# Head of a mixer kernel: one x tile ahead of w1, two tiles through DMA transposes, second products as single groups

## The chip, the cores and the metric

The kernel runs on one core of a Trainium2 chip. The metric is the device time of one execution in microseconds (us). The time before is 138.96 us, the median of 3 runs (138.89 to 139.11). A core has five engines that run side by side, each through its own list of instructions in order: TensorE (PE; its weight loads are listed as PEld), VectorE (DVE), ScalarE (ACT), GpSimd (POOL) and SyncE (SP), whose queue issues nearly all DMAs here. They wait for each other through semaphores.

## The reference

x has 2048 rows (tokens) of 512 numbers, in bf16.

```python
h  = gelu(layernorm(x) @ w1)                  # 512 -> 512
c  = 128                                      # four channel groups, each shifted along the rows
g0 = h[:, :,   0:128] shifted down by 1 row   # zeros come in at the end
g1 = h[:, :, 128:256] shifted up by 1
g2 = h[:, :, 256:384] shifted down by 2
g3 = h[:, :, 384:512] shifted up by 2
x1 = x + concat(g0, g1, g2, g3) @ w2          # 512 -> 512
out = x1 + gelu(layernorm(x1) @ w3) @ w4      # 512 -> 1792 -> 512
```

## The kernel before, in words

**Tiles.** Row 16p + t of x lies in partition p of tile t, so there are 16 tiles of 128 rows, and a shift by one row is a step to the next tile (at the ends also by one partition, for which a few columns of zeros are kept). All of x, of the weights and of the intermediate results stays on the chip.

**First layer.** For a tile, VectorE takes the statistics (step `st`, line 328) and aggregates them to mean and variance (`ag`, 331); GpSimd makes 1/sqrt(variance + eps) by a power (`rs`, lines 354 and 363, for two tiles at once); VectorE normalizes the tile to bf16 (`norm`, 434). Tile 2 is an exception: ScalarE sums it and its squared deviations (`sum`, `dev`, lines 378 and 390), and `vp`, `vpd` and `pw` (lines 407, 399, 414) make its factor and tile 3's. The normalized tile has to be transposed. Either TensorE does it, four 128 by 128 transposes into a PSUM bank (`tp`, 456) and an evacuation to `xT` by ScalarE (`evA`, 468) or VectorE (`evD`, 470); or a DMA transpose, issued by SyncE, does it from SBUF to SBUF (`dT`, 444). Before, tiles 0 to 7 go through TensorE and 8 to 15 through the DMA. The product with w1 (`m1`, 507) is made for pairs of tiles, one or more of the four output groups at a time; tiles 0 and 1 go one by one and input chunk by input chunk (`m1x`, 524), so that they can begin with the first half of w1. ScalarE applies the gelu (`g1`, lines 551 to 568) and writes `hT`, four channel groups with tiles side by side.

**Second product.** `m2 t b j...` (line 582) multiplies, for output tile t into PSUM bank b, the shifted window of channel group j with its rows of w2; four groups j add up in the bank. Tile t wants the gelus of tiles t - 2 to t + 2. VectorE adds x (`add`, 594).

**Second layer.** Statistics, factor, normalization (on ScalarE for the first ten tiles, 424) and a DMA transpose for each tile of x1, in the order 2, 3, ..., 15, 0, 1. Then, for four tiles at a time, the wide product with w3 (line 609, output 1792, gelu at 622) and the narrow one with w4 (line 635), an addition of x1 (649) and the store (653).

**Order.** Nothing is scheduled automatically: the program's steps are recorded in the order of a text, `HEAD`, and of the calls behind it, and each engine runs its instructions in just this order. A helper derives the waits from what each step reads and writes. So a step that waits holds back everything behind it on its engine. The loads of x, w1 and w2 stand first on SyncE's queue, then the DMA transposes of the first layer in the order of `HEAD`, then w3, then the transposes of x1 with the loads of w4 between them, and the stores. TensorE starts with `keep_warm` matmuls on constants (line 667), 12 of them and two more after the statistics of tile 1 (`warm 2 3 1`).

## Time and profile before

| | us |
|---|---|
| median of 3 runs | 138.96 (138.89 to 139.11) |
| the profiled execution | 138.48 |
| its span | 136.6 |
| TensorE busy | 132.6 (97%) |
| ScalarE busy | 51.7 (38%) |
| VectorE busy | 50.9 (37%) |
| GpSimd busy | 18.8 (14%) |

The span is the time from the program's first profiled instruction to its last; all times of the profile are counted from its start. In a row of the timeline stand the start, the duration, the engine, the line of the kernel, the operation, what it writes and reads, and how many instructions were merged; in square brackets the idle time of the engine before it, and what ended that. A duration of a TensorE instruction is its latency: matmuls overlap, and the next one starts before the last is done. The chain that ended last is followed back from the last instruction, at each step to what released it, or else to the instruction before it on its engine; its pieces do not overlap, so they add up to the span. Of a DMA, the profile shows the time of the issue and how long after it the data had landed.

### The profile page before, as it was taken

The page shows a single profiled execution, that of the slowest core. Times are in us where ns is not written, and L with a number is a line of the kernel's source. Part 1 is how long each engine was busy: PE and PEld are TensorE (multiplying, and loading weights), DVE is VectorE, ACT ScalarE, POOL GpSimd, SP SyncE. Part 2 cuts the span into 40 slices and gives each one's busy share as a digit, 9 for nine tenths or more (in the row PEclk, how much of TensorE's full clock was granted, in tenths as well). Part 3 has the DMA queues.
Part 4 walks back from the last instruction along what each step waited for, and adds up shares of the span by engine and source line. Part 5 has one row for each costly group of instructions (what it writes and reads, how often), then busy time and mean ns, then how long its engine had stood idle before and what let it go on. Part 6 is the DMA issues. An engine that isn't in the chain of part 4 may idle for free.

```text
span 136.6 us, 1835 instructions
## 1 busy us (share of the span) xinstructions
PE 132.6 (97%) x716; PEld 67.3 (49%) x716; DVE 50.9 (37%) x125; ACT 51.7 (38%) x64; POOL 18.8 (14%) x52
## 2 busy tenths in 40 slices
PE   7979999999999999999999999999999999999993
PEld 3369857664444444444444444444444444444452
DVE  2699889999966610000322000023200002322222
ACT  4558623499535555552000555200055530000000
POOL 2644431553322200000000000000000000000000
PEclk9999999999999999999999999999999999999999
DMA  4996153499845499300111100011110001111121
GB/s 106 275 307 238 38 101 74 96 286 294 174 96 113 89 268 243 135 5 0 38 38 38 38 5 0 0 38 38 38 38 0 5 0 38 38 38 38 39 78 42
DMA packets 20264, 12.18 MB, mean 89 GB/s; under 512 B 13728, under 2 KB 19104, under 8 KB 20256
## 3 DMA queue, kind: packets, MB, share of 16 engines
q1 hardware_dynamic: 20112, 12.03, 33.3%
q8 instruction: 6, 0.10, 0.3%
q10 hardware_dynamic: 144, 0.03, 0.1%
q14 instruction: 2, 0.02, 0.1%
HBM read 6.82 MB, written 2.10 MB: 65 GB/s over the span
## 4 chain that ended last, share of the span: by engine, by line
PE 93%; DMA 3%; SPq 1%; DVE 1%; issue 0%
PE ps L635 35%; PE ps L609 35%; PE ps L582 10%; PE ps L507 9%; DMA x_sb<-in_x_dram 3%; PE ps L524 1%; PE ps L456 1%; SPq L258 1%; DVE st L328 1%; DVE xn L434 0%; DVE o_sb L649 0%
## 5 line engine op out<-in xcount | busy, mean ns | idle before, releaser
L635 PE MATMUL ps<-w_sb,h2T 128*128 128x512 bf16 (+2 forms) x238 | 48.9, 366 | 0.0
L609 PE MATMUL ps<-x1T,w_sb 128*128 128x512 bf16 x224 | 48.8, 379 | 0.0
L622 ACT ACTIVATE h2T<-ps 128x1024 bf16<-128x1024 f32 x28 | 28.7, 1024 | 44.8 <-PE ps L609 44.8
L649 DVE TENSOR_TENSOR o_sb<-ps,x_sb 128x512 bf16<-128x512 f32 (+2 forms) x17 | 11.2, 660 | 75.0 <-PE ps L635 75.0
L635 PEld LDWEIGHTS ps<-w_sb,h2T 128*128 128x128 bf16 x238 | 22.7, 98 | 26.0
L609 PEld LDWEIGHTS ps<-x1T,w_sb 128*128 128x128 bf16 x224 | 22.0, 98 | 26.4
L328 DVE BATCH_NORM_STATS2 st<-x_sb 128x6 f32<-128x512 bf16 x31 | 20.2, 680 | 2.9 <-DMA x_sb<-in_x_dram 2.9
L582 PE MATMUL ps<-w_sb,hT 128*128 128x512 bf16 x64 | 14.8, 379 | 0.0
L507 PE MATMUL ps<-xT,w_sb 128*128 128x256 bf16 x112 | 13.7, 273 | 0.0
L507 PEld LDWEIGHTS ps<-xT,w_sb 128*128 128x128 bf16 x112 | 10.7, 98 | 2.3 <-ACT xT L468 0.2
L363 POOL TENSOR_TENSOR rstd<-vpe,neghalf 128x2 f32<-128x2 f32 (+1 forms) x16 | 11.2, 699 | 0.9
L594 DVE TENSOR_TENSOR x_sb<-ps,x_sb 128x512 bf16<-128x512 f32 x16 | 10.3, 678 | 0.3 <-PE ps L582 0.2
L434 DVE TENSOR_SCALAR xn<-x_sb,mv,rstd 128x512 bf16<-128x512 bf16 x21 | 8.0, 404 | 4.5 <-POOL rstd L363 4.4
L582 PEld LDWEIGHTS ps<-w_sb,hT 128*128 128x128 bf16 x64 | 6.2, 98 | 6.3 <-ACT hT L568 0.3
L424 ACT ACTIVATE xn<-x_sb,nmr,rstd 128x512 bf16<-128x512 bf16 x10 | 7.5, 808 | 3.3 <-POOL nmr L368 3.3
L568 ACT ACTIVATE hT<-ps 128x1024 bf16<-128x1024 f32 x6 | 6.1, 1020 | 5.6 <-PE ps L507 5.6
L354 POOL TENSOR_SCALAR vpe<-mv 128x2 f32<-128x2 f32 (+1 forms) x16 | 3.7, 230 | 25.9 <-DVE mv L331 25.7
L667 PE MATMUL ps<-const-bfloat16-1.0 128*128 128x512 bf16 x14 | 6.0, 602 | 0.8 <-PEq L817 0.8
L468 ACT ACTIVATE xT<-ps 128x512 bf16<-128x512 bf16 x8 | 4.6, 597 | 2.2 <-PE ps L456 2.2
L331 DVE BATCH_NORM_AGGREGATE mv<-st 128x2 f32<-128x6 f32 x31 | 4.7, 172 | 0.1
L456 PE MATMUL ps<-ident,xn 128*128 128x128 bf16 x32 | 3.2, 231 | 0.9 <-DVE xn L434 0.9
L667 PEld LDWEIGHTS ps<-const-bfloat16-1.0 128*128 128x128 bf16 x14 | 1.9, 144 | 3.5 <-issue 3.5
(27 smaller groups left out, 17.2 us busy)
## 6 DMA issues: line engine op xcount, KB each, us to landing
w_sb<-in_w_dram SPq DMA_DIRECT2D x4, 512.0 KB, 4.4
out_dram<-o_sb SPq DMA_DIRECT2D x15, 128.0 KB, 1.8
w_sb<-in_w_dram SPq DMA_DIRECT2D x1, 1792.0 KB, 8.5
x_sb<-in_x_dram SPq DMA_DIRECT2D x4, 256.0 KB, 5.5
w_sb<-in_w_dram SPq DMA_DIRECT2D x3, 256.0 KB, 4.5
x_sb<-in_x_dram SPq DMA_DIRECT2D x4, 128.0 KB, 2.5
x_sb<-in_x_dram SPq DMA_DIRECT2D x1, 512.0 KB, 7.0
x1T<-xn SPq DMA_TRANSPOSE x16, 2.9
```

The lines of the kernel that those rows point to most:

```text
L328: pr.op("dve", f"st{q}", lambda e: e.bn_stats(st6[:, q, :], a), r=[g], w=[g_st[q]])
L363: lambda e: e.tensor_tensor(rstd[:, q : q + n], vpe[:, q : q + n], neghalf[:, 0:n], ALU.pow),
L424: lambda e: e.activation(xn[:, s, :], a, ACT_F.Identity, bias=nmr[:, q : q + 1], scale=rstd[:, q : q + 1]),
L434: lambda e: e.tensor_scalar(xn[:, s, :], a, mv[:, q, 0:1], rstd[:, q : q + 1], ALU.subtract, ALU.mult),
L507: ins = e.matmul(dst, w1_sb[:, dc, P * fc : P * (fc + 1)], xT[:, dc, 256 * p : 256 * (p + 1)], start=(dc == 0), stop=(dc == DC - 1))
L582: ins = e.matmul(bankap(b), hT[:, j, c : c + P], w2_sb[:, j, :], start=(j == 0), stop=(j == DC - 1))
L594: lambda e: e.tensor_tensor(x1_sb[:, t, :], bankap(b), x_sb[:, t, :], ALU.add),
L609: ins = e.matmul(bankap(b + i), w3_sb[:, dc, P * fc : P * (fc + 1)], x1T[:, dc, 512 * s : 512 * (s + 1)], start=(dc == 0), stop=(dc == DC ...
L622: pr.op("act", f"g2_{s}_{fp}", lambda e: e.activation(o, a, ACT_F.Gelu_apprx_tanh), r=gens, w=[g])
L635: ins = e.matmul(ps[:, 512 * b : 512 * b + n], h2T[:, fc, s % 2, P * i : P * (i + 1)], w4_sb[:, fc, c0 : c0 + n], start=(fc == 0), stop=(f ...
L649: lambda e: e.tensor_tensor(o_sb[:, s, 0:n], ps[:, 512 * b : 512 * b + n], x1_sb[:, t, c0 : c0 + n], ALU.add),
L667: ins = e.matmul(bankap(b), ones[:, 0:P], ones, start=True, stop=True)
```

## The change

It has five parts.

- Loads: tiles 4 and 5 were one transfer of 256 KB ahead of w1. Now tile 4 alone stands there (128 KB), and tile 5 is a transfer of its own behind the two halves of w1.
- Tiles 6 and 7 go through DMA transposes (`dT 6`, `dT 7`) and no longer through TensorE, PSUM and ScalarE. The evacuation of tile 0 moves from ScalarE to VectorE (`evD 0`).
- The fillers: 11 ahead and 3 after the statistics of tile 1, instead of 12 and 2, and the 3 now stand ahead of tile 0's transposes.
- Second products are issued as single groups j in any order. `mm2` counts how many groups of a tile have been issued, so that the first one issued starts the sum in the bank and the fourth ends it.
- Another order of the steps in `HEAD`. Among them: tile 4's statistics come ahead of tile 1's normalization as before, but tile 5's only after the normalizations of tiles 2 and 3; tiles 4 to 7 are normalized in order; the second products begin with tiles 4, 2 and 3, in single groups. Behind `HEAD`, only the groups of tiles 6 and 7 that are left are issued, and w4 comes in two transfers instead of four.

```diff
-st 0; ag 0; rs 0 1; st 1; ag 1; sum 2; st 3; rs 1 1; norm 0; ag 3; tp 0 4; dev 2; vp 3; vpd 2;
-st 4; evA 0; norm 1; warm 2 3 1; pw 2 2; tp 1 5; st 5; m1x 0 0 0; m1x 0 0 1; norm 2; evA 1;
-m1x 0 0 2; norm 3; ag 4; tp 2 6; ag 5; m1x 0 0 3; rs 4; tp 3 7; evA 2; m1x 1 0 0; st 6;
-m1x 1 0 1; m1x 1 0 2; evA 3; m1x 1 0 3; st 7; ag 6; ag 7; m1 1 4 0; rs 6; norm 5; g1 0; norm 4;
-m1 1 4 1; tp 5 7; tp 4 6; st 8; evA 5; norm 7; m1 1 4 2; m1 1 4 3; evA 4; st 9; tp 7 7; ag 8;
-ag 9; rs 8; norm 6; m1 2 0 0; evA 7; m1 2 0 1; st 11; tp 6 6; g1 1; m1 2 0 3; norm 8; ag 11;
-m1 2 0 2; evA 6; m2 2 4 0; st 10; m2 2 4 1; norm 9; ag 10; m1 3 2 1; g1 2; rs 10; m1 3 2 3;
-st 13; m1 3 2 0; st 12; ag 13; m1 3 2 2; norm 11; m2 2 4 2; dT 8; m2 2 4 3; st 14; g1 3; norm 10;
-m2 3 5 0 1 2 3; dT 9; st 15; ag 12; ag 15; ag 14; rs 12; m2 4 6 0 1 2 3; m1 4 0 1; add 2; dT 11;
-m1 4 0 0; rs 14; norm 13; m1 4 0 3; m1 4 0 2; add 3; norm 15; dT 10; norm 14; m2 5 7 0 1 2 3;
-g1 4; norm 12; dT 13; dT 12; dT 15; dT 14
+st 0; ag 0; rs 0 1; st 1; ag 1; sum 2; st 3; rs 1 1; norm 0; ag 3; dev 2; st 4; warm 3 3 1; vp 3;
+tp 0 4; vpd 2; norm 1; evD 0; tp 1 5; ag 4; pw 2 2; m1x 0 0 0; evA 1; m1x 0 0 1; norm 2;
+m1x 0 0 2; norm 3; tp 2 6; m1x 0 0 3; tp 3 7; st 5; evA 2; ag 5; m1x 1 0 0; m1x 1 0 1; rs 4;
+m1x 1 0 2; evA 3; st 6; m1x 1 0 3; m1 1 4 3; st 7; g1 0; ag 6; ag 7; m1 1 4 0; rs 6; norm 4;
+norm 5; tp 4 6; tp 5 7; st 8; evA 4; m1 1 4 1; norm 6; evA 5; m1 1 4 2; st 9; ag 8; ag 9;
+m1 2 0 1; rs 8; norm 7; g1 1; m1 2 0 0; st 10; m1 2 0 2; st 11; m1 2 0 3; m2 4 6 2; norm 9;
+m2 2 4 0; dT 6; m2 4 6 0; m2 3 5 0; st 15; ag 11; g1 2; m2 2 4 1; m2 5 7 2; norm 8; ag 10;
+m2 2 4 2; rs 10; m2 4 6 1; dT 7; m2 2 4 3; st 13; m2 3 5 2; m2 5 7 0; m2 3 5 1; add 2; ag 15;
+m1 3 2 3; norm 10; dT 9; m2 3 5 3; m1 3 2 1; st 12; ag 12; ag 13; m1 3 2 0; rs 12; norm 11; dT 8;
+m1 3 2 2; m2 6 4 2; st 14; m2 6 4 0; m1 4 0 3; add 3; g1 3; norm 12; m1 4 0 0; dT 10; ag 14;
+rs 14; norm 13; m1 4 0 1; m2 5 7 1; m2 7 5 2; m2 4 6 3; m2 5 7 3; dT 11; m2 6 4 1; norm 15;
+m2 7 5 0; norm 14; m1 4 0 2; dT 12; g1 4; dT 13; dT 15; dT 14
...
         def mm2(t, b, js=(0, 1, 2, 3)):
 
             if t not in g_o:
                 g_o[t] = (bank[b].new(), b)
+                n_o[t] = 0
+            n0 = n_o[t]
+            n_o[t] += len(js)
             win = [window(j, t) for j in js]
 
             def f(e):
-                for j, (c, _) in zip(js, win):
+                for n, (j, (c, _)) in enumerate(zip(js, win), n0):
                     ins = e.matmul(bankap(b), hT[:, j, c : c + P], w2_sb[:, j, :],
-                                   start=(j == 0), stop=(j == DC - 1))
+                                   start=(n == 0), stop=(n == DC - 1))
...
-        load_x("sp", 4, 2)
+        load_x("sp", 4, 1)
         load_w("w1", w1_sb, w1, 0, 2)
         load_w("w1", w1_sb, w1, 2, 2)
+        load_x("sp", 5, 1)
         load_x("sp", 6, 2)
...
-        keep_warm(12, 3)
+        keep_warm(11, 3)
...
-        mm2s(4, 4)
+        mm2(6, 4, (3,))
+        mm2(7, 5, (1, 3,))
...
-            load_w4(2 * (k - 10), 4)
+            if k < 14:
+                load_w4(7 * (k - 10) // 2, 7)
         wide(0, [2, 3])
-        load_w4(12, FC - 12)
```

More of the change, by code (lines that the diff above doesn't have):

```diff
@@ L569, in gelu1 @@
                       r=gens, w=[g_h[(j, p)] for j in range(DC)])
-        g_o = {}
+        g_o, n_o = {}, {}
         def mm2(t, b, js=(0, 1, 2, 3)):
```

## The prediction

> **What bounds the kernel now.** I read the page first (busy shares, chain), then the chain in order of time, then TensorE and VectorE over 5 to 15 us, then SyncE's queue and the landing times.

> ```profile
> span 136.6 us, 1835 instructions
> PE 132.6 (97%) x716; PEld 67.3 (49%) x716; DVE 50.9 (37%) x125; ACT 51.7 (38%) x64; POOL 18.8 (14%) x52
> ...
> PE 93%; DMA 3%; SPq 1%; DVE 1%; issue 0%
> ```
> TensorE is the bound. The chain in order of time tells from when:

> ```profile
> 2.58 4.20 DMA x_sb<-in_x_dram
> ...
> 6.80 0.69 DVE st L328
> 7.50 0.33 DVE xn L434
> ...
> 7.87 0.40 PE ps L456 x4
> 8.27 0.67 PE ps L524 x12
> 8.94 0.24 PE ps L456 x4
> ...
> 10.52 0.89 PE ps L507 x8
> 11.41 0.45 PE ps L456 x8
> ...
> 134.24 0.02 issue
> 134.26 0.29 DVE o_sb L649
> ```
> From 7.87 to 134.24 us every piece is TensorE's: the instructions there stand back to back, and their gaps add up to some 0.1 us. So only three things can move the end: TensorE's work, the time at which the dense run begins, and new holes in it. It begins late because tiles 4 and 5, one transfer issued at 2.58, land at 6.78; VectorE takes the statistics of tile 4 before it normalizes tile 1, whose transpose starts the run.

> ```profile
> 6.29 0.71 PE L667 MATMUL ps<-const-bfloat16-1.0 128*128 128x512 bf16 x2
> 7.87 0.40 PE L456 MATMUL ps<-ident,xn 128*128 128x128 bf16 x4 [0.88 <-DVE xn L434]
> 8.10 0.83 PE L524 MATMUL ps<-xT,w_sb 128*128 128x128 bf16 x12
> ```
> ```profile
> 6.80 0.69 DVE L328 BATCH_NORM_STATS2 st<-x_sb 128x6 f32<-128x512 bf16 x1 [0.89 <-DMA x_sb<-in_x_dram]
> 7.41 0.40 DVE L434 TENSOR_SCALAR xn<-x_sb,mv,rstd 128x512 bf16<-128x512 bf16 x1
> ...
> 9.12 1.27 DVE L328 BATCH_NORM_STATS2 st<-x_sb 128x6 f32<-128x512 bf16 x2
> 10.32 0.30 DVE L331 BATCH_NORM_AGGREGATE mv<-st 128x2 f32<-128x6 f32 x2
> 10.53 0.70 DVE L434 TENSOR_SCALAR xn<-x_sb,mv,rstd 128x512 bf16<-128x512 bf16 x2
> ```
> The reader sees both engines wait 0.88 us for that landing, and, in the last three rows, the pace of VectorE's later chain: from the statistics of tile 6 (9.12) to the normalization of the next tile (10.53) 1.41 us. That number decides below.

> **The change part by part.** The sum is made against the profiled execution: 138.48 us, its span 136.6 and 1.9 around it. The median is 138.96, so it lies 0.48 under; I take the difference to the median.

> *Two tiles leave TensorE.* Four transposes of a tile take 0.22 to 0.24 us of the chain. Tiles 6 and 7: **-0.45 us**. Three ScalarE evacuations go with this and the next part (0.60 each, off the path).

> *An earlier start.* Tile 4 alone is 128 KB. Tiles 0 to 3, of that size, land 2.2, 2.5, 2.5 and 2.7 us after their issue; issued at 2.58, tile 4 should land near 5.5 (bounds: 4.8, where tile 3 lands, and 6.78, the pair's). VectorE is free at 5.84 (the aggregation at 5.74), so the statistics run to 6.53 and the normalization of tile 1 to 6.84: the engine, not the landing, now sets this, until tile 4 comes after 5.8. On TensorE the fillers stand at 12 in 5.28 us, starting 0.43 apart from 0.76: 11 and 3 more, now ahead of the first transpose, end near 6.6 (the last falls to 0.33, as the one at 6.29 did). Tile 0's transposes follow to 6.84 with the result at 7.0; tile 1's fit in before 7.1. The evacuation of tile 0 has moved to VectorE, and everything waits for it: the first product (line 524's group), and behind it on VectorE the normalizations of tiles 2 and 3. No row shows a 16-bit copy out of PSUM there. The nearest rows are 0.40 (normalization, from SBUF) and 0.68 (the addition out of PSUM, f32, two inputs); ScalarE takes 0.60 for the same copy. I take 0.55, so it runs 7.04 to 7.6 and the first product starts at 7.65 instead of 8.10. The first half of w1 landed at 7.5 (issued at 3.06, 4.4 us) and doesn't bind even unmoved; the second at 8.2 and is wanted at 8.1, where half a pair less ahead of it is worth more than the 0.1. **-0.45**; with 0.40 and 0.68, -0.6 and -0.3.

> [...]

> *New holes.* TensorE runs through both tiles' first products and half of pair 1 (16 + 16 matmuls of 128 columns, the transposes of tiles 2 and 3, 8 of line 507) and stands before tile 4's transposes at 10.77. They wait for normalization 4, and VectorE gets there only after the statistics of tiles 5, 6 and 7. With S the start of tile 6's statistics: normalization 4 at S + 1.41, its end 0.40 later, transposes of tile 4 at S + 1.87, of tile 5 to S + 2.41; ScalarE evacuates 4 and 5 one after the other (0.50 apart, 0.60 the last); pair 2 starts at S + 3.44. Without any wait it would start at 12.09 (10.77, two tiles 0.45, two groups 0.87). What is S? VectorE alone: normalization 3 ends near 8.3, statistics and aggregation of tile 5 take 0.8, so 9.04. The transfer: tile 6 landed at 9.1 (issued at 4.04, 5.0 us), and in the new order exactly as many bytes stand ahead of it; that gives 9.1 to 9.2. I take S = 9.15: pair 2 at 12.59, holes of 0.50 against some 0.07 in this stretch before: **+0.43**.

> Sum: -0.45 - 0.45 + 0.43, rounded by the walk's own steps to -0.45: **138.5 us** (the execution 138.0, span 136.15). Each 0.1 us of S is 0.1 us of time. The floor, S = 9.04, is -0.55, or -0.58 with the fast copy.

> *SyncE's queue.* The transposes stand 1.30 us apart (four issues in 5.19), and land 2.5 us after issue:

> ```profile
> 14.86 11.31 SPq L444 DMA_TRANSPOSE xT<-xn  x8
> 26.21 0.58 SPq L265 DMA_DIRECT2D w_sb<-in_w_dram  x1
> ```
> Now ten: the one of tile 6 waits for normalization 6, at 12.2, with all other transposes and w3 behind it. Tile 7 then lands at 16.1; pair 3 is wanted at 16.9: cover 0.8. Pair 4 is covered by 0.6, pair 6 by 0.6. The tenth ends at 25.5, so w3 is issued at about 25.6 instead of 26.21 and lands (8.5 us) at 34.1 to 34.7; the four x1 transposes of the first wide stage land half a us apart behind it, the last at 36.2 to 36.8, where TensorE arrives at 36.9 (before: 31.71 + 5.1 = 36.8 against 37.33). No cost, with 0.1 to 0.7 of cover.

> *Single second products, new order.* The 64 matmuls of line 582 stay 64, at 0.216 (before, single ones stand at 14.95 with 0.43 for two): nothing. They start at 14.3 rather than 14.79 and need w2, landed at 13.8: cover 0.5. The additions, statistics and gelus of this stretch leave at least 0.2 us of cover in my walk through the order. w4 as two loads of 7 chunks, near 43.5 and 46.8, each some 4.4 us to landing, is wanted at 61.2: nothing.

> **The rivals.**

> *Small transfers pay each for itself: no change.* Tiles 1, 2 and 3 land 0.77, 0.47 and 0.64 us apart, 1.88 for 384 KB, where w1's second half and tile 6 come 0.73 and 0.88 after their forerunners with 256 KB each. Two tiles at 0.63 instead of one pair at 0.8 put tile 6 at 9.1 + 0.46 = 9.56, S at 9.59: holes of 0.94, time 138.96. For it: the early rows. Against: from 5 us on the DMA engines' share is 0.78 or more in every half us, so bytes should count. [...]

> *Tile 6 lands as the ninth transfer: slower.* It is now the ninth issue. The ninth before, tiles 8 and 9 at 4.55, landed after 6.0 us, at 10.53. Then S is 10.55, pair 2 starts at 13.99, and the time is 139.9. It decides from a landing at 9.85 on. Against: that one had 256 KB more ahead of it.

> *A transpose lands late: slower or the same.* Of the eight before, one (issued at 20.63) took 3.3 us, the others 2.5. A delay of 0.8 on the second tile of pair 6 or 3 passes the cover by 0.2; twice that, as tile 6's comes while w2 is still landing, by 1.0: 138.7 to 139.5.

> **How the numbers follow.** What a measurement of this kernel can tell from no change is 0.2%, 0.28 us. Forecast (S up to 9.3): 0.54. Small transfers: 0.22, of which a fifth is still faster or already slower. Ninth transfer: 0.13. Late transposes: 0.11, mostly slower. Faster 0.55, same 0.20, slower 0.25. The range goes from the floor with 0.1 us of scatter, 138.3, to the late cases, 139.4; the forecast's own is 138.35 to 138.7.

> **What would show it.** Right: tile 4's statistics start before 6, line 525's first matmul near 7.65, two or three holes of TensorE between 10.7 and 12.6 that add up to 0.5, released by normalization 4 and the evacuation of tile 5, and none from there on; the wide stage starts near 36.9. Wrong: tile 6 landing after 9.4, a hole that a DMA transpose, w2 or w3 ends, or a copy on VectorE above 0.7.

## The result

The changed kernel is slower: 139.47 us against 139.06 us for the kernel before, medians of 18 runs each; the ratio is 1.0043, with a 95% interval of 1.0024 to 1.0063. The forecast was 138.5, faster. The profiled execution of the change, 141.12 us with a span of 139.2, is the longest of its 18; two more profiles were therefore taken (139.44 and 139.22 us, spans 137.6 and 137.4), and what is said of the change below is what all three show, unless it names one. The profile of before (138.48) lies at the other side, 0.6 under the median of the 18 runs of its kernel.

The page of the change: TensorE does less, and yet the span is longer, since the chain holds DMAs and VectorE where before, from 7.87 us on, it held TensorE alone.

```profile
span 139.2 us, 1820 instructions
PE 132.3 (95%) x708; PEld 66.3 (48%) x708; DVE 51.4 (37%) x126; ACT 50.0 (36%) x61; POOL 18.9 (14%) x52
...
PE 79%; DMA 11%; DVE 5%; SPq 2%; issue 1%; DVEq 0%
```

The chain of the same execution in order of time (start, duration, what):

```profile
4.56 5.46 DMA x_sb<-in_x_dram
...
10.04 1.29 DVE st L329 x2
...
17.25 4.27 DMA xT<-xn
...
21.56 1.48 PE ps L508 x12
...
34.26 5.55 DMA x1T<-xn
...
39.95 24.33 PE ps L613 x112
...
136.88 0.29 DVE o_sb L653
```

Three transfers stand in it: tile 6, which lands at 10.02; a DMA transpose of the first layer that takes 4.27 us instead of 2.5; and the x1 transposes behind w3. From the start of the wide stage (39.95; before 37.33 in TensorE's timeline) to the last addition it is 96.93 us in both kernels. So the whole loss arises ahead of that stage. TensorE's timeline of this execution shows where it stands still, in square brackets:

```profile
11.90 0.72 PE L457 MATMUL ps<-ident,xn 128*128 128x128 bf16 x8 [1.12 <-DVE xn L435]
...
21.56 1.48 PE L508 MATMUL ps<-xT,w_sb 128*128 128x256 bf16 x12 [1.10 <-DMA xT<-xn]
...
39.95 1.24 PE L613 MATMUL ps<-x1T,w_sb 128*128 128x512 bf16 x5 [0.65 <-DMA x1T<-xn]
```

The first hole was forecast (with 0.5 us for it and its neighbours), the second and third were not. The third stands in this profile alone: w3, which is issued ahead of the x1 transposes, landed at 37.7 here and at 34.6 and 34.5 in the other two. (A hole's idle time in brackets counts from the modelled end of the last matmul; from start to start the second is 1.27 us longer than the streams need.)

### The profile page after: what moved, and what is told of

It reads as the page before. It is cut to its first block, busy times and chain, and to the rows that moved or that the text cites. A ratio compares the mean times of both kernels' runs of the same rounds, so it can differ in the third digit from the quotient of the medians.

```text
span 139.2 us, 1820 instructions
## 1 busy us (share of the span) xinstructions
PE 132.3 (95%) x708; PEld 66.3 (48%) x708; DVE 51.4 (37%) x126; ACT 50.0 (36%) x61; POOL 18.9 (14%) x52
## 4 chain that ended last, share of the span: by engine, by line
PE 79%; DMA 11%; DVE 5%; SPq 2%; issue 1%; DVEq 0%
PE ps L613 35%; PE ps L639 35%; PE ps L508 5%; DMA x1T<-xn 4%; DMA x_sb<-in_x_dram 4%; PE ps L586 4%; DVE st L329 3%; DMA xT<-xn 3%; SPq L259 2%; DVE xn L435 1%; SPq L266 1%; DVE mv L332 0%; DVE o_sb L653 0%; DVE x_sb L598 0%; DVEq L134 0%
## 5 line engine op out<-in xcount | busy, mean ns | idle before, releaser
L508 PEld LDWEIGHTS ps<-xT,w_sb 128*128 128x128 bf16 x112 | 10.7, 98 | 4.1 <-DMA xT<-xn 1.6
L671 PE MATMUL ps<-const-bfloat16-1.0 128*128 128x512 bf16 x14 | 5.0, 518 | 0.9 <-PEq L823 0.8
L457 PE MATMUL ps<-ident,xn 128*128 128x128 bf16 x24 | 2.3, 221 | 1.7 <-DVE xn L435 1.7
L469 ACT ACTIVATE xT<-ps 128x512 bf16<-128x512 bf16 x5 | 2.8, 595 | 3.1 <-PE ps L457 3.1
```

What stands on the lines that cost most here:

```text
L508: ins = e.matmul(dst, w1_sb[:, dc, P * fc : P * (fc + 1)], xT[:, dc, 256 * p : 256 * (p + 1)], start=(dc == 0), stop=(dc == DC - 1))
L671: ins = e.matmul(bankap(b), ones[:, 0:P], ones, start=True, stop=True)
```

## The experiments

Two theories were set against each other at first. LOAD: tile 6 lands late, and VectorE's chain opens the holes ahead of pair 2. QUEUE: with two more transposes in a row ahead of w3, transposes and w3 are late.

**The two kernels again**, without an edit.

> The changed kernel as it is, for a second profile, since the first one (141.12 us) is the longest of its 18 times and the median is 139.47. Theory LOAD (tile 6 lands late and VectorE's chain opens holes in TensorE ahead of pair 2; each 0.1 us later than 9.59 costs 0.1): the statistics of tile 6 start at 9.9 to 10.1 again, pair 2's first product near 13.4, the wide stage starts at 37.6 to 37.9, and no hole that a DMA transpose ends is over 0.3 us. Rival QUEUE (two more transposes in a row ahead of w3; a delayed one delays the rest and w3, and the wide stage waits): tile 6's statistics near 9.2, w3 issued after 27, and the wide stage's start is ended by an x1 transpose that lands after 38.

> The kernel before as it is, for a second profile: both theories expect tile 6's statistics at 9.1 (9.0 to 9.3), TensorE dense from 7.9 to 8.1 on and the wide stage at 37.3 to 37.6, with no wait for a transpose.

The change took 139.44 us. Tile 6 landed at 9.4, tile 5 at 8.7; pair 2's first product came at 13.05 and the wide stage at 38.4. Neither theory holds as it was put: the holes ahead of pair 2 are there (1.05 us from start to start), but ahead of pair 3 stands another that a transpose ends, while w3 is no cause here. TensorE's timeline:

```profile
18.45 0.60 PE L508 MATMUL ps<-xT,w_sb 128*128 128x256 bf16 x4 [0.90 <-DMA xT<-xn]
```

The kernel before took 139.26 us: even it is not always dense. The second half of w1 landed at 9.25, not 8.2, TensorE waited 0.92 us for it, and the wide stage began at 38.2 where 37.3 to 37.6 was expected. So the landings in the head move by up to 1.1 us from profile to profile (w1's second half here, tile 6 in the change); this is why one profile of each doesn't give the difference.

In each profile of the change one transpose of the first layer takes over 4 us (min, median and max of the ten in this second profile, a window of 12 to 26.5 us):

```profile
DMA to landing us min/median/max: 2.5/2.5/4.2
```

What the late ones have in common shows in the DMA view of the time just behind their issue, here 15 to 16.8 us of this second profile (first row: busy tenths in 40 slices; last row: the two issues in the window, with their median time to landing; the one issued at 14.13 took 4.19, the next one 3.62):

```profile
DMA  0000900025899999989989999999000000000000
...
q8 instruction: 1, 0.02, 5.2%
...
xT<-xn SPq DMA_TRANSPOSE x2, 3.9
```

A load of 16 KB of instructions (queue q8; its share of 16 engines over 1.8 us makes 1.5 us on one engine) falls among the transposes. In the first profile of the change it is the same load, at 18.3, and the DMA engines' rate drops to nearly nothing for 1.5 us soon behind it (window, busy us of each engine, granted clock, DMA share, GB/s; a packet counts with all its time where it starts, so a share can exceed 1):

```profile
18.50:19.00 0.50, 0.50 (x7) 0.40 (x5) 0.50 (x2) 0.00 (x0) 0.00 (x0) 1.00 0.92 183
19.00:19.50 0.50, 0.50 (x7) 0.46 (x5) 0.47 (x4) 0.00 (x0) 0.00 (x0) 1.00 2.45 61
19.50:20.00 0.50, 0.50 (x6) 0.42 (x5) 0.50 (x2) 0.00 (x0) 0.37 (x2) 1.00 0.03 3
20.00:20.50 0.50, 0.46 (x3) 0.00 (x0) 0.50 (x2) 0.43 (x1) 0.50 (x1) 1.00 0.08 9
20.50:21.00 0.50, 0.00 (x0) 0.00 (x0) 0.50 (x2) 0.50 (x1) 0.12 (x1) 1.00 0.11 18
21.00:21.50 0.50, 0.00 (x0) 0.00 (x0) 0.50 (x3) 0.09 (x1) 0.05 (x1) 1.00 0.99 194
```

The packets tell why. An undisturbed transpose is 512 packets of 256 bytes, and moves them in 0.7 to 0.8 us. Of the late one, 478 had begun by 19.4, with the load of instructions still running (18.28 to 19.87); the other 34 follow from 19.8 to 20.7, nearly one at a time. The window 19.75 to 20.65:

```profile
DMA packets 30, 0.01 MB, mean 9 GB/s; under 512 B 30, under 2 KB 30, under 8 KB 30
...
q1 hardware_dynamic: 30, 0.01, 7.5%
```

A sixteenth of 512 is 32, the share of one of the 16 DMA engines if the packets are spread evenly, and 7.5% of 16 engines over 0.9 us is 1.1 us of one engine. So the late rest looks like the share of the one engine that had to fetch the instructions first; the trace does not name a packet's engine, so this is a reading of the counts. The second profile has the same picture, 479 and 33 packets. The next transpose's packets begin only when these are through (20.9), so it is late as well (3.63 us).

In the two profiles of the kernel before, this load stands at 13.4 and 14.2 us, about where the last load lands (13.8 and 13.9) and ahead of the first transpose (14.86 and 15.71), so no transpose is in flight. That gave the third theory, FETCH: the load of instructions, where it meets a transpose, makes it late.

**The loads back, and tiles 6 and 7 back on TensorE**, each alone.

```diff
-        load_x("sp", 4, 1)
+        load_x("sp", 4, 2)
...
-        load_x("sp", 5, 1)
```

> The changed kernel with its loads as before: tiles 4 and 5 in one transfer ahead of w1. LOAD: the first product moves back to 8.0 to 8.1, but tile 6's statistics start near 9.1 instead of 10.0, so pair 2 starts near 13.0 instead of 13.4 and the time falls by 0.3 to 0.5 us against the change, to about that of the kernel before. QUEUE: the transposes and w3 stand as in the change, so the time stays within 0.2 us of the change (139.4 to 139.6 beside a kernel before of 139.06).

139.55 us, a ratio to the kernel before of 1.0044 (1.0016 to 1.0072): as slow as the change itself, as QUEUE had it. LOAD's gain isn't there. In its profile the instruction load came at 18.15, one transpose took 4.25 us, and a hole of 1.22 us opened ahead of pair 4.

```diff
-m1 2 0 1; rs 8; norm 7; g1 1; m1 2 0 0; st 10; m1 2 0 2; st 11; m1 2 0 3; m2 4 6 2; norm 9;
-m2 2 4 0; dT 6; m2 4 6 0; m2 3 5 0; st 15; ag 11; g1 2; m2 2 4 1; m2 5 7 2; norm 8; ag 10;
-m2 2 4 2; rs 10; m2 4 6 1; dT 7; m2 2 4 3; st 13; m2 3 5 2; m2 5 7 0; m2 3 5 1; add 2; ag 15;
+m1 2 0 1; rs 8; norm 7; g1 1; m1 2 0 0; tp 6 7; evA 6; st 10; m1 2 0 2; st 11; m1 2 0 3; tp 7 7; evA 7; m2 4 6 2; norm 9;
+m2 2 4 0; m2 4 6 0; m2 3 5 0; st 15; ag 11; g1 2; m2 2 4 1; m2 5 7 2; norm 8; ag 10;
+m2 2 4 2; rs 10; m2 4 6 1; m2 2 4 3; st 13; m2 3 5 2; m2 5 7 0; m2 3 5 1; add 2; ag 15;
```

> The changed kernel with tiles 6 and 7 through TensorE and ScalarE again, so that eight transposes stand ahead of w3. QUEUE: w3 is issued near 26.3 and the wide stage no longer waits; the time falls to that of the kernel before (139.0) or at most 0.3 above it. LOAD: TensorE has 0.45 us more to do and the same holes ahead of pair 2; the time is 0.4 to 0.8 us above the change, 139.9 to 140.3 beside a kernel before of 139.06.

139.26 us, ratio 1.0019 (0.9988 to 1.005): 0.32 above the kernel before, at the edge of what QUEUE expected and well under LOAD's. It does not tell QUEUE from FETCH, though: here the transposes begin at 15.25 and the instruction load at 15.8; it meets the first one only, which takes 3.20 us, and no transpose ends a hole.

**The load of instructions moved, and nothing else.** Each filler matmul of 512 columns becomes four of 128 (or two of 256): the same columns in the same time (TensorE is 5.0 us busy with them in the first profile of the change, and 5.0 in one with quarters), with 84 (or 28) more instructions in front. This was meant to bring the program earlier to the place of the load.

```diff
-                for _ in range(n):
-                    ins = e.matmul(bankap(b), ones[:, 0:P], ones, start=True, stop=True)
+                for i in range(4 * n):
+                    c = 512 * b + P * (i % 4)
+                    ins = e.matmul(ps[:, c : c + P], ones[:, 0:P], ones[:, 0:P],
+                                   start=True, stop=True)
```

> The changed kernel with each filler of 512 columns made of four of 128: the same columns and time ahead of the data, but 84 more TensorE instructions in front. Theory FETCH (a 16 KB load of TensorE's instructions on queue q8 falls among the first layer's DMA transposes, as at 15.2 and 18.3 us in the two profiles of the change, and holds one of them 1.7 us longer, which opens a hole of 1.1 to 1.3 us ahead of pair 3 or 4): the load now comes at 10 to 12, ahead of the first transpose near 12.8 to 13.3; all ten take 2.4 to 2.6 us but one that the 8 KB load on q14 near 22 meets (3.0 to 3.4); no hole that a transpose ends is over 0.4; the time falls by 0.7 to 1.1 us against the change (139.5), to 138.4 to 138.8. Rival QUEUE (ten transposes in a row are late for themselves, wherever the instructions are loaded): the hole of 1.1 to 1.3 stays, time 139.3 to 139.7.

138.46 us; ratio to the kernel before 0.9978 (0.9956 to 1.0000). The load came at 12.8, later than the 10 to 12 expected, but ahead of the transposes' data. From the second transpose on all ten took 2.4 to 2.6 us, the first 3.57, and no transpose opened a hole. This profile (139.24, the longest of the 12) shows what the moved load can cost instead: w2 landed at 15.6 rather than 14.1, and TensorE stood 1.2 us ahead of the second products. Whether the load held w2 up is not shown.

> The changed kernel with each filler as two of 256 columns, 28 more TensorE instructions. FETCH: the load moves by some 1.5 us only, to 13.5 to 17, still among the transposes (from 12.8 on) or just at their beginning; one of them takes about 4.2 us, tile 6's, 7's or 9's, and the hole ahead of pair 3 or 4 stays between 0.7 and 1.3. QUEUE: the same hole as in the change, ahead of pair 3 or 4.

138.79 us, one run. The load came at 13.0, still ahead of the first transpose's data; none of the ten waits for it (one takes 3.35, beside the 8 KB load at 21.7), and no transpose ends a hole. The expectation of a late transpose failed: in this one run 28 instructions were as good as 84.

> The kernel before with the same 84 more TensorE instructions. FETCH: its load of instructions came at 13.4 to 14.2, ahead of its first transpose at 14.9 to 15.7, and now comes at 9 to 11 among the loads of x; its transposes stay as they were, and so does the time, within 0.3 us. QUEUE: the same.

138.80 us, ratio 0.9990 (0.9962 to 1.0018): no change, as expected. The load came at 12.84. But the transposes did not stay as they were: the second 16 KB load came forward too, from 31.2 and 35.3 to 25.5, and met the seventh transpose, which took 4.00 us. No hole followed.

**The reverse: a load among the transposes of the kernel before.** On top of the quarter fillers, the first products of pairs 1 to 3 are made in halves.

```diff
-                    dst = ps[:, 512 * b + 256 * fc : 512 * b + 256 * (fc + 1)]
-                    for dc in range(DC):
-                        ins = e.matmul(dst, w1_sb[:, dc, P * fc : P * (fc + 1)],
-                                       xT[:, dc, 256 * p : 256 * (p + 1)],
-                                       start=(dc == 0), stop=(dc == DC - 1))
+                    k = 2 if p < 4 else 1
+                    for h in range(k):
+                        m = 256 // k
+                        o = 512 * b + 256 * fc + m * h
+                        for dc in range(DC):
+                            ins = e.matmul(ps[:, o : o + m], w1_sb[:, dc, P * fc : P * (fc + 1)],
+                                           xT[:, dc, 256 * p + m * h : 256 * p + m * (h + 1)],
+                                           start=(dc == 0), stop=(dc == DC - 1))
```

> The kernel before with the quarter fillers and, besides, the first products of pairs 1 to 3 in halves of 128 columns: 96 more TensorE instructions and at 2.5 ns for each extra matmul 0.12 us more. FETCH: the second 16 KB load of instructions (31 to 35 us before) moves to 17 to 20, among the eight transposes; one of them takes 4 to 4.3 us instead of 2.5, a hole of 0.5 to 1.3 us opens ahead of pair 4, 5 or 6, where before has none, and the time rises by 0.6 to 1.3 us to 139.6 to 140.3. QUEUE: eight transposes have their old cover; no hole, time up by 0.1 to 0.2.

139.32 us, ratio 1.0029 (1.0008 to 1.0051); 0.52 us above the kernel before with quarter fillers, of which 0.12 are by estimate the 48 extra matmuls, at 2.5 ns each (in the chain of before, 12 matmuls of 128 columns take 0.67 us and 112 of 512 columns 24.17, so four of 128 take 7.5 ns more than one of 512). That is less than the 0.6 to 1.3 expected. The second 16 KB load came at 17.4, the transpose issued at 16.41 took 3.94 us, and the old kernel, with its eight transposes, its loads of x and its order, has the hole. The DMA view from 16.4 to 19 us, and TensorE's timeline:

```profile
DMA  8999999974100009000269999999999090001000
...
q8 instruction: 1, 0.02, 3.3%
```

```profile
20.48 1.69 PE L510 MATMUL ps<-xT,w_sb 128*128 128x256 bf16 x14 [0.85 <-DMA xT<-xn]
```

So neither ten transposes nor the new loads of x were needed for this hole of 0.85 us; a load of instructions in the midst of the transposes was enough.

**On one chip: the change as it is, with quarter fillers, and its parts without the load in the way.** The first two have no new edit.

> The changed kernel as it is, beside the three below on the same chip, and a third profile. FETCH: 0.3 to 0.6 us above the kernel before; the 16 KB load of instructions starts after 15 and holds a transpose of the first layer for 3.6 to 4.3 us. QUEUE: the same time, and a late transpose without that load beside it.

139.24 us, ratio 1.0031 (1.0004 to 1.0058). The load at 15.0 for the third time met the transposes, and the one issued at 13.95 took 4.09 us:

```profile
18.17 0.60 PE L508 MATMUL ps<-xT,w_sb 128*128 128x256 bf16 x4 [0.69 <-DMA xT<-xn]
```

> The changed kernel with the quarter fillers again, for an interval on the same chip as the change itself. FETCH: 0.7 to 1.1 us under the change and 0.3 to 0.6 under the kernel before; no hole that a transpose ends. QUEUE: as the change, within 0.3 us.

138.56 us, 0.68 under the change on the same chip, where 0.7 to 1.1 was expected (the twelve runs lie at 138.06 to 138.98, those of the change at 138.42 to 139.72). To the kernel before the ratio is 0.9990 (0.9964 to 1.0015): only 0.12 under it, where 0.3 to 0.6 was expected. The load came at 12.3. In this profile pair 2 starts at 12.94, as in the third profile of the change (12.88); pair 3, which stood at 18.17 there, comes 0.89 earlier, without a wait:

```profile
17.28 0.60 PE L508 MATMUL ps<-xT,w_sb 128*128 128x256 bf16 x4
```

That is nearly all of the 0.96 us by which the two profiled executions differ (139.22 and 138.26). The chain from the transposes of tiles 4 and 5 on is TensorE's alone:

```profile
10.93 0.31 DVE xn L435
...
11.28 0.72 PE ps L457 x8
...
12.94 1.91 PE ps L508 x16
...
37.40 24.17 PE ps L613 x112
```

Here, too, the second 16 KB load met a transpose, the tenth (25.5; 3.97 us), and no hole followed.

The next kernel has two of the edits shown above together: the fillers in quarters, and tiles 6 and 7 back on TensorE.

> Quarter fillers, and tiles 6 and 7 through TensorE again. With the load of instructions out of the way of the transposes, the part of the change that takes these tiles off TensorE should show its own worth: by the prediction's term 0.45 us (8 transposes of a quarter of 0.22 us each tile's four), and some 0.2 more for places where TensorE now waits for their evacuations. FETCH: 0.3 to 0.7 us above the changed kernel with quarter fillers. QUEUE (transposes in a row are the cost): not above it, rather 0.3 to 1.0 under it.

138.87 us, ratio 1.0026 (1.0001 to 1.0052); 0.31 above the change with quarter fillers, at the lower end of what FETCH expected and against QUEUE. All twelve runs (from 138.72) lie above the other's median. Without the load in the way, the DMA transposes of tiles 6 and 7 are a gain.

The last one has the fillers in quarters and the loads as before.

> Quarter fillers, and the loads as before (tiles 4 and 5 in one transfer ahead of w1). The first product moves from 7.3 to 7.5 back to 7.6 to 8.1, but the holes ahead of pair 2 follow tile 6, which with the pair lands at 8.8 to 9.1 and alone at 9.2 to 10.0. Theory LOAD: this is worth as much as the earlier start or more: 0 to 0.4 us under the changed kernel with quarter fillers. Against it, the prediction's own step (the split is worth 0.45 us less the holes): 0.1 to 0.4 above it.

138.77 us, ratio 1.0015 (0.9991 to 1.0038); 0.21 above the change with quarter fillers, with intervals that overlap, so the sign is not shown. The first product moved back to 7.78, the holes ahead of pair 2 shrank to 0.33, and the second half of w1, at 8.79 in this profile, cost 0.6. The split of the load is worth little in either direction.

## Why the prediction was wrong

**The step that failed** is the one on SyncE's queue: a transpose lands 2.5 us after issue, so pair 3 has 0.8 us of cover and pair 4 has 0.6, and nothing is lost. In all three profiles of the change one transpose of those two pairs took 4.1 to 4.3 us, 1.6 to 1.8 more, because 16 KB of instructions were loaded beside it; that opened a hole of 0.86 to 1.27 us. Moving the load alone brought the time to 138.46 and 138.56, and moving one into the transposes of the kernel before cost that kernel 0.4.

The 16 KB load was in the trace of before too, at 13.4, and cost nothing, as no transpose was in flight. The change begins its transposes at 12.6 to 13.3 instead of 14.9, while its load comes at 15.0 to 18.3, in the midst of them; why later than in the kernel before, isn't settled. The rival "a transpose lands late" had the place right, with 0.11 for its chance, and its range, 138.7 to 139.5, even holds the result. That is luck: its 0.8 was read from the one transpose of before that took 3.3 (beside a smaller load of instructions, 8 KB on q14 at 22.5), and its doubling was laid to w2 for tile 6, whose transpose took 2.5 to 2.7 in all three.

**The earlier start** came out larger: the first product at 7.24 to 7.42, not 7.65 (8.10 before, but 7.76 in its second profile). Tile 4 landed at 5.1 to 5.7, the fillers ended near 5.9 instead of 6.6, and VectorE's copy out of PSUM took 0.42 us where 0.55 was taken, nearer the 0.40 of the normalization than the 0.68 of the addition. No run shows the term for a fast copy in the floor (-0.58 instead of -0.55); what the runs showed is this copy of 0.42 and S, the start of tile 6's statistics, at 9.39 to 10.04. The earlier start gained nothing at the end, since pair 2 waited for S (next step).

**The new holes ahead of pair 2** were at the forecast place, released by normalization 4 and the evacuation of tile 5, but 0.69, 1.05 and 1.60 us long instead of 0.50. Pair 2 began at 12.88, 13.05 and 13.57, where 12.59 was forecast: 0.3 to 1.0 lost. Its distance from S was forecast as 3.44 and came out as 3.5 in all three. What was wrong is S: 9.39, 9.57 and 10.04 instead of 9.15. In the longest profile it is tile 6, which landed at 10.0, and in the second tile 5 (8.7). In the third neither is waited for (they landed at 8.25 and 8.88), and S is VectorE's own:

```profile
7.92 0.41 DVE L430 TENSOR_SCALAR xn<-x_sb,nmean,rstd 128x512 bf16<-128x512 bf16 x1 [0.47 <-POOL rstd L415]
...
9.39 1.25 DVE L329 BATCH_NORM_STATS2 st<-x_sb 128x6 f32<-128x512 bf16 x2
```

VectorE waits 0.47 us for GpSimd's factor of tile 2, in each profile of the change. The prediction has no such wait, which is why its floor, S = 9.04, was too low: with the fillers in quarters S is 9.45 and 9.46, again without a wait for a landing. The landing itself was well forecast: over the eight profiles with tile 5 as a transfer of its own, tile 6 landed between 8.6 and 10.0, half of them before 9.22, where 9.1 to 9.2 was taken.

**Two tiles off TensorE**, -0.45 by the sum, measured 0.31 between two kernels without the load in the way. **Small transfers** (the rival for no change): tile 6 landed 0.6 to 1.8 us after tile 5 in the three profiles, but after the 9.56 of this rival in only two of the eight; it is not borne out as the usual case.

**The third profile as a sum**: start 0.68 earlier, transposes 0.45 less, holes 1.93 in all (0.29 ahead of tile 2's transposes, which wait for the same factor of GpSimd, 0.69, 0.86, and some 0.1 at the landing of w2), gives +0.80; its wide stage begins at 38.18, 0.85 after that of the profile before. The medians differ by only 0.4 because the profile of before, against which the sum was made, was a lucky one: it has none of the 0.92 us that its second profile lost to w1.

Without the load in the way the time is 138.46 and 138.56, where 138.5 was forecast, but against the kernel before on the same chip that is 0.51 and 0.12 less. Whether the rest of the change gains the 0.45 of the sum is open.

## What to carry to other kernels

A row of DMA transposes with 0.6 to 0.8 us of cover was not covered here, where one of them took 4.1 to 4.3 us instead of 2.5. Look in the trace for the loads of instructions, list when they come in the kernel as it is, and ask whether the edit, by moving transfers or by changing the number of instructions in front, brings the two together. Where they meet, a few instructions more ahead of that place can move the load: 28 and 84 did here (from 15.0 to 18.3 to 12.3 to 13.0), and the kernel before lost no time by 84 (ratio 0.9990). But they moved a later load as well (in the kernel before from 31.2 and 35.3 to 25.5), and that one met another transpose, which took 4.00 us. And where a head depends on the times at which loads land, take more than one profile before a sum is set against it; ask, too, which engine's result ends last once the landing is earlier.

## What the runs showed of the hardware

That these are TensorE's instructions is inferred from what moved them: nothing but more TensorE instructions. What sets their moment stays open: with 28 or with 84 more instructions the first load came at 12.3 to 13.0, whereas in the change as it is it came at 15.0, 15.2 and 18.3, although its program was the same each time.
